# Attention scores as 64 by 64 tiles of the matrix array, with queries loaded contiguous

## The chip, the cores and the metric

The kernel runs on one core of a Trainium2 chip. The metric is device time in microseconds (us) of one execution, the median of several runs. PE is the matrix engine (PEld its weight loads), DVE, ACT and POOL are the vector, scalar and general engines, SP issues most of the transfers.

## The reference, cut to what matters

Three stages follow each other: attention over a window of 64 positions, a feed-forward layer with a rational activation, and a gated linear unit. All of it is float32.

```python
# q, k, v: (4, 8, 576, 64): batch, heads, positions, head size
scores = scale * np.matmul(q, k.transpose(0, 1, 3, 2))      # scale = 1/8
rel = pos[:, None] - pos[None, :]
mask = (rel >= 0) & (rel < 64)
attn = softmax(np.where(mask, scores, -1e9))                # over the keys
x = heads_joined(np.matmul(attn, v))                        # (2304, 512)

h = x @ w_in                                                # (2304, 2048)
g = (a0 + a1*h + a2*h*h + a3*h*h*h) / (1 + |b0|*|h| + |b1|*h*h + 1e-6)
x2 = g @ w_out                                              # (2304, 512)

out = (sigmoid(x2 @ w_gate) * (x2 @ w_val)) @ w_out2        # d_ff = 1536
```

A query sees itself and the 63 positions ahead of it. So the 64 queries of one chunk of a sequence (576 positions are 9 chunks) need the 128 keys of two chunks: the one before and their own.

## The kernel before, in words

The 2304 tokens are cut into 18 units of 128 tokens, `u` = 0 to 17, and these into five blocks of 512, 384, 384, 512 and 512 tokens (units 0 to 3, 4 to 6, 7 to 9, 10 to 13, 14 to 17). `unit` writes down the attention of one unit; `step1` and `step2` write down the two feed-forward stages of a block, one slice of 128 of the hidden width at a time. Weights come in raw, are taken apart into a high and a low float32r part by ACT, DVE and POOL (names `wraw`, `wt`, `wb`, `w`), and three matmuls (`mm3`, line 744) replace one in float32. In the first phase the second product of a slice is a plain float32 matmul (line 842).

The order of the work is made ahead of time. Each call of `op` records a piece of work with a priority, the engines that can do it with a cost each, and what it needs. `Plan.order` then plays the kernel through with these costs, and emits each piece on the engine and at the place that it finds: so a piece's cost or priority moves others, too. On the chip each engine runs its pieces strictly in that order.

The attention of a unit takes these steps, with the eight heads as four pairs (`HP` = 4; a pair fills 128 partitions, 64 for each head):

- `load_qk` loads queries and keys (SP; the first block's keys from ACT's queue). The queries of a pair and of one chunk of 64 tokens form a 128 by 128 square with the two heads on its diagonal. Off the diagonal it is zero: `off_diagonal` clears those quarters with POOL memsets, in four buffers `qd` for the first block and in one, `q_diag`, for all later units, where they stay zero. The load fills the diagonal in two transfers, each a 64 by 8 by 64 block with runs of 256 bytes.
- `scores(m)` makes the scores of chunk m of the unit (m = 0, 1): four float32 matmuls of 128 by 128 by 128 (line 592), one for each pair of heads, into one bank of PSUM. The rows of the result are 2 heads by 64 queries, its columns the 128 keys. In units 0 to 6 (`on_pe`) a bfloat16 matmul of the mask with the identity (line 590) goes into the bank first; later units add the mask on DVE (`mask`, line 599).
- `peak`, `exps`, `inverse`, `norm` are the softmax (DVE, ACT, DVE, POOL or DVE; lines 607 to 629). `turn` transposes on PE (line 640) up to unit 9, `blocks` on DVE (line 657) from unit 10 on.
- `values` multiplies with v (line 666): 16 float32 matmuls of 128 by 64 by 64, whose results go to partitions 0 to 63 and 64 to 127 in turn, so that each uses one half of the columns of the array.
- `x_hi`, `x_lo` take the result apart into the input of `step1`.

A float32 matmul stands as two records of a weight load and a MATMUL in the trace, so the 4 matmuls of a scores job are 8 records. The pool `a` of PSUM has two banks: scores, transposes and values of units from 4 on use them, as do the val product of `step2` and weights that are taken apart late. Where PE has nothing to do before the first feed-forward matmul, the planner fills in matmuls on a cleared tile (`warm`, line 385).

## Time and profile before

| | |
|---|---|
| median of 3 runs | 958.29 us (957.88 to 958.46) |
| span of the profiled execution | 957.6 us, 13934 instructions |
| PE busy | 936.7 us, 98% of the span |
| DVE, ACT, POOL busy | 687.1, 480.9, 276.4 us |
| chain that ended last, by engine | PE 88%, DVE 6%, ACT 3% |

The profile is that of one execution. Its span runs from the first to the last instruction; its own time was not recorded apart from that, and the median of the runs is 0.7 us above the span. A record's start is observed, the end of a MATMUL is modelled, so the time that a job takes on a busy PE is read from where the next job starts. Busy time is the union of an engine's records.

### The profile page before, as it was taken

To read this page: it belongs to the slowest core of one execution; us is meant where nothing else is said; L and a number is where in the kernel's file an instruction comes from. 1 tells how busy PE (TensorE), PEld (TensorE's weight loads), DVE (VectorE), ACT (ScalarE), POOL (GpSimd) and SP (SyncE) were. 2 spreads that over 40 slices of the span, in tenths; PEclk is the share of its full clock that TensorE was granted. 3 is DMA by queue.
4 is the path that set the end of the run, shared out by engine and by line. 5 is a ranking of instruction groups with operands and counts; after the bars stand their busy time and mean duration, and the time that the engine had idled before them with its cause. 6 is when DMAs were issued, how large, how long until landed. Compare 5 with 4: busy or idle time off the path is not lost.

```text
span 957.6 us, 13934 instructions
## 1 busy us (share of the span) xinstructions
PE 936.7 (98%) x4984; PEld 794.0 (83%) x4984; DVE 687.1 (72%) x1174; ACT 480.9 (50%) x983; POOL 276.4 (29%) x286
## 2 busy tenths in 40 slices
PE   8899988999999999999999999999999999999998
PEld 7756646888899999989999998888888888888886
DVE  6999999999999898886667775988998632222221
ACT  6878875567688776753234435544666310001001
POOL 5576653333465343311111112344312000000000
PEclk9999999999999999999999999999999999999999
DMA  9977898999991257953138873100455520013001
GB/s 265 389 249 246 277 315 307 312 364 327 310 358 46 98 165 253 297 165 100 34 94 282 284 237 129 45 1 23 137 195 197 176 66 23 0 44 110 1 1 44
DMA packets 77476, 166.71 MB, mean 174 GB/s; under 512 B 24992, under 2 KB 34208, under 8 KB 77408
## 3 DMA queue, kind: packets, MB, share of 16 engines
q1 hardware_dynamic: 75296, 164.79, 50.8%
q10 hardware_dynamic: 2112, 1.05, 0.5%
q8 instruction: 39, 0.64, 0.3%
q14 instruction: 29, 0.24, 0.1%
HBM read 121.24 MB, written 44.56 MB: 173 GB/s over the span
## 4 chain that ended last, share of the span: by engine, by line
PE 88%; DVE 6%; ACT 3%; DMA 1%; issue 1%; POOL 1%; DVEq 0%; POOLq 0%; ACTq 0%
PE h L744 34%; PE y L744 30%; PE a L744 14%; PE y L842 4%; DVE et L657 2%; PE a L592 2%; PE a L666 2%; ACT sm L615 1%; DMA cb_raw<-in_moe_b_dram 1%; PE a L385 1%; DVE tg L793 1%; DVE wt L444 0%; PE a L640 0%; DMA qd<-in_q_dram 0%; DVE wt L449 0%
## 5 line engine op out<-in xcount | busy, mean ns | idle before, releaser
L744 PE MATMUL h<-x,w 128*128 128x512 f32 (+1 forms) x1680 | 374.6, 372 | 5.2 <-DVE x L322 1.4
L744 PEld LDWEIGHTS h<-x,w 128*128 128x128 f32 x1680 | 306.9, 188 | 53.4 <-issue 3.6
L744 PE MATMUL y<-g,w 128*128 128x384 f32 (+1 forms) x768 | 163.5, 362 | 0.6 <-POOL g L327 0.6
L744 PE MATMUL a<-x,w 128*128 128x512 f32 (+1 forms) x720 | 158.8, 369 | 0.0
L744 PE MATMUL y<-w,g 128*128 128x512 f32 x648 | 158.6, 392 | 0.0
L934 ACT ACTIVATE sg<-h 128x512 f32<-128x512 f32 (+1 forms) x60 | 33.4, 556 | 238.6 <-PE h L744 236.8
L744 PEld LDWEIGHTS y<-g,w 128*128 128x128 f32 x768 | 138.8, 188 | 16.3 <-POOL g L327 1.1
L744 PEld LDWEIGHTS a<-x,w 128*128 128x128 f32 x720 | 130.6, 188 | 16.9
L744 PEld LDWEIGHTS y<-w,g 128*128 128x128 f32 x648 | 120.4, 188 | 24.1
L793 DVE SCALAR_TENSOR_TENSOR tg<-tg,ca_sb,h 128x512 f32<-128x512 f32 (+1 forms) x160 | 110.0, 690 | 19.1 <-ACT ta L772 13.3
L937 DVE TENSOR_TENSOR sg<-sg,a 128x512 f32<-128x512 f32 (+1 forms) x60 | 37.9, 632 | 118.6 <-PE a L744 118.0
L790 POOL TENSOR_TENSOR tq<-tq,ta 128x512 f32<-128x512 f32 (+1 forms) x56 | 75.5, 1348 | 52.6 <-ACT tq L781 39.5
L799 ACT ACTIVATE tr<-tq,biases 128x512 f32<-128x512 f32 (+1 forms) x80 | 54.2, 679 | 57.2 <-POOL tq L790 48.5
L776 ACT ACTIVATE tg<-h,ca_sb 128x512 f32<-128x512 f32 (+1 forms) x80 | 51.6, 645 | 41.9 <-PE h L744 41.4
L824 DVE SCALAR_TENSOR_TENSOR tg<-tg,ca_sb,tr 128x512 f32<-128x512 f32 (+1 forms) x80 | 67.2, 842 | 1.4 <-POOL tr L821 1.2
L805 DVE SCALAR_TENSOR_TENSOR tq<-tq,tr 128x512 f32<-128x512 f32 (+1 forms) x80 | 56.8, 711 | 11.8 <-ACT tr L802 9.2
L441 POOL TENSOR_SCALAR wraw<-wraw 128x512 f32<-128x512 f32 x55 | 45.8, 840 | 58.4 <-ACT wt L428 38.8
L842 PE MATMUL y<-tg,w 128*128 128x512 f32 x128 | 57.5, 594 | 2.9 <-DVE tg L824 2.8
L657 DVE STREAM_TRANSPOSE et<-sm 32x256 f32<-32x256 f32 x128 | 55.8, 436 | 2.2
L802 ACT ACTIVATE tr<-tr,biases 128x512 f32<-128x512 f32 (+1 forms) x80 | 54.2, 679 | 1.6
L785 POOL TENSOR_SCALAR tq<-ta,cb_sb 128x512 f32<-128x512 f32 (+1 forms) x31 | 25.0, 808 | 94.6 <-ACT ta L772 90.2
L322 DVE CAST g<-sg 128x512 fp32r<-128x512 f32 (+1 forms) x31 | 15.2, 490 | 48.6 <-PE y L744 48.5
(105 smaller groups left out, 1063.9 us busy)
## 6 DMA issues: line engine op xcount, KB each, us to landing
w<-wp SPq DMA_DIRECT2D x30, 512.0 KB, 3.4
wraw<-in_moe_w_out_dram SPq DMA_DIRECT2D x28, 512.0 KB, 6.0
w<-wv SPq DMA_DIRECT2D x26, 512.0 KB, 3.5
w<-wg SPq DMA_DIRECT2D x25, 512.0 KB, 3.5
w<-wo SPq DMA_DIRECT2D x19, 512.0 KB, 3.7
vv<-in_v_dram SPq DMA_DIRECT2D x35, 256.0 KB, 4.2
wraw<-in_moe_w_in_dram SPq DMA_DIRECT2D x16, 512.0 KB, 8.3
wi<-w SPq DMA_DIRECT2D x16, 512.0 KB, 3.1
```

What stands on the lines that cost most here:

```text
L441: nc.gpsimd.tensor_scalar(out=x, in0=x, scalar1=0.0, scalar2=0.0, op0=ALU.mult, op1=ALU.mult)
L657: nc.vector.transpose(out=to[cols, :, rows], in_=at[rows, :, cols])
L744: nc.tensor.matmul(p, lhs(a), rhs(b), start=first and n == 0, stop=last and n == 2)
L776: nc.scalar.activation(out=z["g"], in_=z["h"], func=AF.Copy, scale=ca_sb[:, 3:4])
L790: ENGINES[e].tensor_tensor(out=z["q"], in0=z["q"], in1=z["a"], op=ALU.mult)
L793: return lambda e: nc.vector.scalar_tensor_tensor(out=z["g"], in0=z["g"], scalar=ca_sb[:, m:m + 1], in1=z["h"], op0=ALU.add, op1=ALU.mult)
L799: nc.scalar.activation(out=z["r"], in_=z["q"], func=AF.Ln, scale=LN_SCALE, bias=lnb)
L802: nc.scalar.activation(out=z["r"], in_=z["r"], func=AF.Exp, scale=-1.0, bias=exb)
L805: nc.vector.scalar_tensor_tensor(out=z["q"], in0=z["q"], scalar=1.0 + 1e-6, in1=z["r"], op0=ALU.add, op1=ALU.mult)
L824: nc.vector.scalar_tensor_tensor(out=z["g"], in0=z["g"], scalar=ca_sb[:, 0:1], in1=z["r"], op0=ALU.add, op1=ALU.mult)
L842: nc.tensor.matmul(yacc[b][m][:, :n], w[:, m * P:(m + 1) * P], z["g"], start=f == first_f, stop=f == last_f)
L937: nc.vector.tensor_tensor(out=z["t"], in0=z["t"], in1=z["v"], op=ALU.mult)
```

## The change

The scores of a unit are made in another shape. In place of four matmuls of 128 by 128 by 128 for each chunk there are sixteen for the unit, each of one head (64 partitions, `d`) and one chunk (64 queries, `r`): 64 by 64 weights, 128 keys moving. Head j of a pair sits in partitions 64j to 64j+63, so it uses that half of the array's rows, and goes to its own bank; chunk c goes to partitions 64c to 64c+63 of the bank, and so uses that half of the columns. In units 0 to 6 the two heads are still two jobs, in later units one job that takes both banks at once and goes round the four tiles. The queries are loaded as they lie, one transfer of 128 by 512 with runs of 2 KB for each unit, and nothing is cleared. The masks of a bank now hold two chunks, so there are three of them, `nn`, `fn` and `nf`. A table `SHIFTS` adds a number to the priority of 80 pieces of work.

```diff
+SHIFTS = {
+    17: 6, 20: -7, 39: -4, 58: -3, 66: -4, 70: -4, 76: -6, 77: -8, 109: 2.6, 149: -2, 156: -7, 184: -28, 200: -6,
...
-            o.key = (o.prio, n)
+            o.key = (o.prio + SHIFTS.get(n, 0), n)
...
-    q_diag = const.tile([P, 2 * HP, P], F32, name="q_diag")
+    q_sb = const.tile([P, HP, P], F32, name="q_sb")
...
-        nc.vector.tensor_copy(masks["f"], m)
-        nc.vector.memset(masks["f"][:, 0:64], MASKED)
+        for name, c in (("fn", 0), ("nf", 64)):
+            nc.vector.tensor_copy(masks[name], m)
+            nc.vector.memset(masks[name][c:c + 64, 0:64], MASKED)
         nc.vector.tensor_copy(ident16, ident)
-
-    def off_diagonal(engine, tile):
-        for j in range(2):
-            engine.memset(tile[64 * j:64 * j + 64, :, 64 * (1 - j):64 * (2 - j)], 0.0)
...
-            for r in (slice(0, 64), slice(64, P)):
-                nc.sync.dma_start(out=z["q"][r, :, r], in_=qu[r].rearrange("p (n t) -> p n t", t=64))
+            nc.sync.dma_start(out=z["q"], in_=q[:, HP * c0:HP * (c0 + P)].rearrange("p (i t) -> p i t", t=P))
...
-        def scores(m):
+        chunks = [2 * u + c for c in range(2)]
+        mask_u = masks["".join("n" if c % (S // 64) else "f" for c in chunks)][:, None, :].to_broadcast([P, HP, P])
+
+        def scores(js):
...
-                p = z["p", m] = bank(s_s[m])
-                if on_pe:
-                    nc.tensor.matmul(p, ident16, mask_of(m), start=True, stop=False)
+                for j in js:
+                    z["p", j] = bank(s_s[j])
+                    if on_pe:
+                        nc.tensor.matmul(z["p", j], ident16, mask_u, start=True, stop=False)
                 for i in range(HP):
-                    nc.tensor.matmul(
-                        p[:, i * P:(i + 1) * P], z["q"][:, 2 * i + m], z["k"][:, i, 64 * m:64 * m + P],
-                        start=not on_pe, stop=not on_pe or i == HP - 1,
-                    )
+                    for c in range(2):
+                        r = slice(64 * c, 64 * c + 64)
+                        for j in js:
+                            d = slice(64 * j, 64 * j + 64)
+                            nc.tensor.matmul(
+                                z["p", j][r, i * P:(i + 1) * P], z["q"][d, i, r], z["k"][d, i, 64 * c:64 * c + P],
+                                start=not on_pe, stop=not on_pe or i == HP - 1,
+                            )
...
-                            z["et"][:, c, i, 64 * j:64 * j + 64],
+                            z["et"][:, j, i, 64 * c:64 * c + 64],
...
-            o = sc = op(
-                t(j), [pe(512, 4 + on_pe)], scores(j), [lk, zeros, sc, gate],
-                [s_s[j]] + [sm_s][j:], {q_s, k_s}, None if first_block or j else prev_k.get("t"),
-            )
+            if on_pe:
+                sc = op(
+                    t(j), [("PE", 1.4)], scores((j,)), [lk, sc, gate], [s_s[j]] + [sm_s][j:], {q_s, k_s},
+                    None if first_block or j else prev_k.get("t"),
+                )
+            elif j == 0:
+                sc = op(t(0), [("PE", 1.15)], scores((0, 1)), [lk, gate], [*s_s, sm_s], {q_s, k_s}, prev_k.get("t"))
+            o = sc
```

Lines behind the edits shift: the feed-forward matmuls stand at 745 and 843 in place of 744 and 842.

Three places show what moves. The first is SP's queue at the start of the program; `qd` and `q` are the queries of the first block, `ca_sb` and `cb_raw` the coefficients of the rational function, and a bracket names the earlier transfer that a transfer waits for. Before:

```order
L552 DMA qd<-in_q_dram 64x8x64 x4
L373 DMA ca_sb<-in_moe_a_dram 128x4 [waits DMAHW0_49]
L374 DMA cb_raw<-in_moe_b_dram 128x2 [waits DMAHW1_49]
L552 DMA qd<-in_q_dram 64x8x64 [waits DMAHW2_49]
L552 DMA qd<-in_q_dram 64x8x64 [waits DMAHW3_49]
```

And in the changed kernel:

```order
L556 DMA q<-in_q_dram 128x512 x2
L378 DMA ca_sb<-in_moe_a_dram 128x4
L379 DMA cb_raw<-in_moe_b_dram 128x2
L556 DMA q<-in_q_dram 128x512 [waits DMAHW0_49]
L556 DMA q<-in_q_dram 128x512 [waits DMAHW1_49]
```

Two transfers stand ahead of the coefficients in place of four, and the coefficients wait for no earlier transfer.

The second place is PE's order where the first phase of block 0 ends (lines 842 and 843 are its last products) and its second phase begins (`x_1526` and `x_1516` are its input); the scores and transposes between them belong to units 4 and 5. Before:

```order
L842 MATMUL y<-tg,w 128x512 x4
L640 MATMUL a<-ident,sm 128x128 x8
L590 LDWEIGHTS ident_97
L590 MATMUL a<-maskn,ident_97 128x512
L592 MATMUL a<-kt,q_diag 128x128 x4
L590 LDWEIGHTS ident_97
L590 MATMUL a<-maskn,ident_97 128x512
L592 MATMUL a<-kt,q_diag 128x128 x4
L842 MATMUL y<-tg,w 128x512 x4
L744 MATMUL h<-x_1526,w 128x512 x12
```

And in the changed kernel:

```order
L843 MATMUL y<-tg,w 128x512 x4
L640 MATMUL a<-ident,sm 128x128 x4
L843 MATMUL y<-tg,w 128x512 x4
L640 MATMUL a<-ident,sm 128x128 x4
L586 LDWEIGHTS ident_97
L586 MATMUL a<-masknn,ident_97 128x512
L592 MATMUL a<-kt,q_sb 64x128 x8
L586 LDWEIGHTS ident_97
L586 MATMUL a<-masknn,ident_97 128x512
L592 MATMUL a<-kt,q_sb 64x128 x8
L745 MATMUL h<-x_1516,w 128x512 x12
```

The last product has moved up between the two transposes of unit 4, and the scores of unit 5 have moved behind it, next to the first matmul of the second phase.

The third place is PE's order at unit 7, the first without the mask on PE, in the second phase of block 0 (`h` and `a` are the gate and val products, `y` the output product). Before:

```order
L744 MATMUL a<-x_1526,w 128x512 x12
L592 MATMUL a<-kt,q_diag 128x128 x4
L744 MATMUL y<-w,g 128x512 x12
L592 MATMUL a<-kt,q_diag 128x128 x4
L744 MATMUL h<-x_1526,w 128x512 x12
L666 MATMUL a<-et,vv 64x64 x16
```

And in the changed kernel:

```order
L745 MATMUL h<-x_1516,w 128x512 x12
L592 MATMUL a<-kt,q_sb 64x128 x16
L745 MATMUL y<-w,g 128x512 x24
L666 MATMUL a<-et,vv 64x64 x16
L745 MATMUL a<-x_1516,w 128x512 x12
```

Two jobs of 4 matmuls with a product between them have become one job of 16, and 24 matmuls of an output product follow it before a bank of `a` is written again.

## Rows read from the trace of the kernel before

**Rows 1.** The page, busy time, share of the span and instructions of each engine.

```profile
PE 936.7 (98%) x4984; PEld 794.0 (83%) x4984; DVE 687.1 (72%) x1174; ACT 480.9 (50%) x983; POOL 276.4 (29%) x286
```

**Rows 2.** Windows of 24 us: busy us and records of each engine, clock, DMA share.

```profile
24.00:48.00 24.00, 21.24 (x173) 17.65 (x172) 23.58 (x35) 19.78 (x36) 13.08 (x14) 1.00 0.98 389
...
48.00:72.00 24.00, 21.78 (x66) 13.04 (x65) 21.63 (x33) 18.28 (x31) 17.05 (x15) 0.93 0.72 249
...
120.00:144.00 24.00, 20.05 (x68) 10.63 (x66) 22.42 (x36) 17.66 (x41) 13.56 (x13) 1.00 0.92 314
144.00:168.00 24.00, 20.68 (x91) 15.46 (x92) 22.61 (x43) 13.88 (x35) 8.62 (x7) 1.00 0.83 306
...
192.00:216.00 24.00, 24.00 (x149) 19.96 (x148) 22.20 (x38) 15.88 (x42) 7.58 (x8) 1.00 0.98 365
```

**Rows 3.** Timeline of PE: start, us, line, record, count [idle before].

```profile
197.09 1.15 PE L666 MATMUL a<-et,vv 128*64 128x64 f32 x32
198.17 3.02 PE L744 MATMUL y<-w,g 128*128 128x512 f32 x12
201.03 2.89 PE L744 MATMUL a<-x,w 128*128 128x512 f32 x12
203.75 0.60 PE L640 MATMUL a<-ident,sm 128*128 128x128 f32 x4
...
210.15 1.05 PE L592 MATMUL a<-kt,q_diag 128*128 128x128 f32 x8
...
213.78 1.05 PE L592 MATMUL a<-kt,q_diag 128*128 128x128 f32 x8
```

**Rows 4.** Line 666 from 196 to 199 us: record ns min/median/max, first and last start.

```profile
L666 PE MATMUL a<-et,vv x32: 222/222/270, 197.1 to 198.0; 128*64 128x64 f32 x32
```

**Rows 5.** Groups by shape: busy us, mean ns | idle before.

```profile
L629 DVE TENSOR_TENSOR sm<-sm,su 128x512 f32<-128x512 f32 x20 | 14.0, 698 | 0.5
L599 DVE SCALAR_TENSOR_TENSOR sm<-a,maskn 128x512 f32<-128x512 f32 x20 | 13.7, 683 | 5.0 <-PE a L592 5.0
```

**Rows 6.** Timeline of all engines from 0 to 11 us.

```profile
0.73 2.75 SPq L552 DMA_DIRECT2D qd<-in_q_dram  x4
...
2.63 0.59 DVE L361 COPY maskf<-maskn 128x128 bf16<-128x128 bf16 x1 [1.54 <-POOL maskn L357]
...
4.96 0.34 SPq L374 DMA_DIRECT2D cb_raw<-in_moe_b_dram  x1
5.05 0.63 PE L590 MATMUL y<-maskf,ident 128*128 128x512 bf16 x1
...
6.93 1.13 PE L592 MATMUL y<-qk,qd 128*128 128x128 f32 x8 [1.25 <-DMA qd<-in_q_dram]
...
8.83 0.17 DVE L609 TENSOR_SCALAR mx<-mx 128x4 f32<-128x4 f32 x1
...
10.61 0.20 ACT L1047 ACTIVATE cb_sb<-cb_raw 128x2 f32<-128x2 f32 x1 [6.34 <-DMA cb_raw<-in_moe_b_dram]
10.72 0.35 ACT L615 ACTIVATE sm<-y,mx 128x128 f32<-128x128 f32 x1
```

**Rows 7.** DMA issues of the page: KB each, median us from issue to landing.

```profile
vv<-in_v_dram SPq DMA_DIRECT2D x35, 256.0 KB, 4.2
```

**Rows 8.** Timeline of PE from 48 to 155 us.

```profile
53.54 4.14 PE L744 MATMUL h<-x,w 128*128 128x512 f32 x10 [0.37 <-DVE w L327]
...
142.15 0.63 PE L640 MATMUL a<-ident,sm 128*128 128x128 f32 x4 [1.56 <-DVE sm L629]
144.45 0.66 PE L640 MATMUL a<-ident,sm 128*128 128x128 f32 x4 [1.67 <-POOL sm L629]
...
147.46 3.70 PE L842 MATMUL y<-tg,w 128*128 128x512 f32 x8
...
152.56 0.50 PE L744 MATMUL h<-x,w 128*128 128x512 f32 x1 [1.40 <-DVE x L322]
154.40 2.80 PE L744 MATMUL h<-x,w 128*128 128x512 f32 x11 [1.34 <-DVE x L327]
```

More of the change, by code (lines that the diff above doesn't have):

```diff
@@ L58 @@
 HOP = {e: dict(zip(HOP, h)) for e, h in HOP.items()}
+SHIFTS = {
[7 rows of a table added]
+}
 class Plan:
@@ L331, in tile_window_attention__rational_ffn__glu @@
     ident16 = const.tile([P, P], BF16, name="ident16")
-    masks = {m: const.tile([P, P], BF16, name=f"mask{m}") for m in ("n", "f")}
-    q_diag = const.tile([P, 2 * HP, P], F32, name="q_diag")
+    masks = {m: const.tile([P, P], BF16, name=f"mask{m}") for m in ("nn", "fn", "nf")}
+    q_sb = const.tile([P, HP, P], F32, name="q_sb")
     ca_sb = const.tile([P, 4], F32, name="ca_sb")
@@ L348, in constants @@
         nc.vector.memset(two, 2.0)
-        m = masks["n"]
+        m = masks["nn"]
         nc.vector.memset(m, 0.0)
@@ L360, in constants @@
             )
-        nc.vector.tensor_copy(masks["f"], m)
-        nc.vector.memset(masks["f"][:, 0:64], MASKED)
+        for name, c in (("fn", 0), ("nf", 64)):
+            nc.vector.tensor_copy(masks[name], m)
+            nc.vector.memset(masks[name][c:c + 64, 0:64], MASKED)
         nc.vector.tensor_copy(ident16, ident)
-    def off_diagonal(engine, tile):
-        for j in range(2):
-            engine.memset(tile[64 * j:64 * j + 64, :, 64 * (1 - j):64 * (2 - j)], 0.0)
-    def clear_diagonal(e):
-        off_diagonal(ENGINES[e], q_diag)
     def coefficients(e):
@@ L544, in load_qk @@
         def load_qk(e):
-            qu = q[:, HP * c0:HP * (c0 + P)]
             if first_block:
+                z["q"] = tile_of(q_s, [P, HP, P], name="q")
                 z["k"] = spare[0][:, :, c0:c0 + 64 + P]
             else:
-                z["q"] = q_diag
+                z["q"] = q_sb
                 z["k"] = tile_of(k_s, [P, HP, 64 + P])
-            for r in (slice(0, 64), slice(64, P)):
-                nc.sync.dma_start(out=z["q"][r, :, r], in_=qu[r].rearrange("p (n t) -> p n t", t=64))
+            nc.sync.dma_start(out=z["q"], in_=q[:, HP * c0:HP * (c0 + P)].rearrange("p (i t) -> p i t", t=P))
             if first_block:
@@ L568, in load_v @@
             nc.sync.dma_start(out=z["v"][:, 1], in_=v[c0:c0 + P, :])
-        def take_q(e):
-            z["q"] = tile_of(q_s, [P, 2 * HP, P], name="qd")
-        def clear(e):
-            off_diagonal(ENGINES[e], z["q"])
-        def mask_of(m):
-            name = "n" if (2 * u + m) % (S // 64) else "f"
-            return masks[name][:, None, :].to_broadcast([P, HP, P])
-        def scores(m):
+        chunks = [2 * u + c for c in range(2)]
+        mask_u = masks["".join("n" if c % (S // 64) else "f" for c in chunks)][:, None, :].to_broadcast([P, HP, P])
+        def scores(js):
             def go(e):
-                if m == 0:
+                if 0 in js:
                     z["sm"] = tile_of(sm_s, [P, 2, HP, P], name="sm")
@@ L600, in mask @@
                 out=z["sm"][:, c], in0=z["p", c].rearrange("p (i t) -> p i t", i=HP), scalar=scale,
-                in1=mask_of(c), op0=ALU.mult, op1=ALU.add,
+                in1=mask_u, op0=ALU.mult, op1=ALU.add,
             )
@@ L690, in t @@
             return t0 + x
-        ready = zeros = cleared
-        if first_block:
-            ready = op(-360 + u, [("NONE", 0.0)], take_q, [taken], [q_s])
-            zeros = op(-350 + u, [("POOL", 1.1, *PORT)], clear, [ready], uses=[q_s])
         lk = op(
-            prio_load, [dma((1690 if first_block else 1792) * 4 * P, 2.6 if first_block else 3)], load_qk, [ready, near],
-            [x for x in (q_s, k_s) if not first_block], {q_s, k_s}, prev_k.get("k"),
+            prio_load, [dma((1690 if first_block else 1280) * 4 * P, 1.6 if first_block else 2)], load_qk,
+            [taken if first_block else None, near], [q_s] if first_block else [q_s, k_s], {q_s, k_s}, prev_k.get("k"),
         )
@@ L702, in unit @@
         tu = []
-        sc, tr = None, None
+        tr = None
+        sc = None
         for j in range(2):
-            o = sc = op(
-                t(j), [pe(512, 4 + on_pe)], scores(j), [lk, zeros, sc, gate],
-                [s_s[j]] + [sm_s][j:], {q_s, k_s}, None if first_block or j else prev_k.get("t"),
-            )
+            if on_pe:
[6 more added lines that the diff above has]
+            o = sc
             if not on_pe:
@@ L1042, in tile_window_attention__rational_ffn__glu @@
     taken = op(-300, [("NONE", 0.0)], take_spare, takes=[spare_slot])
-    cleared = op(-60, [("POOL", 2.0, *PORT)], clear_diagonal)
     for u in range(UB[0]):
```

6 rows, old and new, of the table SHIFTS are left out of this document.

## The prediction, made before the changed kernel ran

> **What bounds the kernel now.** I read the page first, for which engine is full. PE is busy for 98% of the span [rows 1], so only what shortens PE's own work, or the waits in its missing 2%, can move the end. Next the windows of 24 us over the whole span, for where those 2% lie; five of the 40 stand here [rows 2]. PE lacks 2.8 and 2.2 us in the two windows from 24 us, 4.0 and 3.3 us in the two from 120 us. From 168 us on the windows are full, as the one from 192 us, but for scraps and the end, and what PE saves there comes off the end, if the others keep up. DVE is the one to watch: 23.6 of 24 us busy in the window from 24 us, still 22.2 in the one from 192 us. ACT and POOL have room throughout. So early on DVE and PE share the bound, later PE stands alone.
>
> **Scores in units 7 to 17, the main term.** The reader needs what a job costs on a full PE, from start to start. Twelve 512-column matmuls of the feed-forward take 203.75 - 201.03 = 2.72 us [rows 3]. A scores job of before and the twelve of the product behind it take 213.78 - 210.15 = 3.63 us, so the job costs 0.91, a record of it 0.114, and the two jobs of a unit 1.82 us.
>
> The new shape, 64 by 64 weights with 128 columns moving, is nowhere in the trace. Its nearest row is that of the values, which use half of the array's columns in turn: they and twelve matmuls take 201.03 - 197.09 = 3.94 us, so values cost 1.22 us [rows 3]. Their group lasts 1.15 us, and its last record 0.22 of this, so the 32 starts lie within 0.93 us [rows 3, 4]; the other 0.29 us go into entering and leaving. A record of 64 columns should take half of 0.114 us; 32 in a row would need 1.82, and start within half of that. So the two column halves do work at the same time, at full gain.
>
> The new job has 16 matmuls, 32 records of 128 columns. The bounds: if all four tiles overlap, 32 x 0.114 / 4 = 0.91, and with 0.29 for entering and leaving 1.20 us. If only two do, 1.82 + 0.29 = 2.11. If none do, 3.65 + 0.29 = 3.94. I take 1.20: column halves overlap in the row of the values, and the two row halves here read other partitions and write other banks, so nothing that the column halves share is shared more. That saves 0.62 us a unit, 11 x 0.62 = 6.8 us. Eight of these units lie where PE alone is full; units 7 to 9 lie where DVE has some 2 us free in 24.
>
> The rule that speaks against the change is that of the Trainium skill, "TensorEngine Tiling (Array Packing)", section Tiling Modes: a change of the tiling mode drains the engine. The trace agrees in that the values pay 0.29 us beside their records. By the rule alone, without that price, the sum could not be made; by the row it is in the sum already.
>
> **Scores with the mask on PE, units 0 to 6.** Here a job holds one head, so one row half, and only columns can overlap: 16 records x 0.114 / 2 + 0.29 = 1.20 us against 0.91, 0.29 us more for each job (the mask matmul ahead is unchanged). If nothing overlaps, 2.11, 1.2 us more. The two jobs of unit 6 stand in full PE work: +0.6. The four of units 4 and 5 lie in the stretch from 126 to 155 us, where PE waits for other engines anyway; I count them at nothing, 1.2 us if those waits are gone. Of the eight in block 0 only the first is on the path.
>
> **The start.** The first exponential runs at 10.72 us on ACT, though its row maximum is ready at 8.83 + 0.17 = 9.00 us [rows 6]. What ends last is `cb_raw`: ACT stands in order at the absolute value of it until 10.61, since SP issues it at 4.96, behind four query transfers and a wait for an earlier one. In the new order two transfers stand ahead and no wait. Two issues at 2.75 / 4 = 0.69 us each (the price of the four now), and one of 0.34 ahead of it, bring it to some 2.5 us; with the same 10.6 - 5.0 = 5.6 us on its way it is there at 8.1. The first scores wait until 6.93 for the second query transfer. One of 256 KB takes 4.2 us from issue to landing where it is v [rows 7], so 4.9, and the mask matmul, which ends at 5.05 + 0.63 = 5.68, is then the last. So scores 1.25 us earlier, 0.29 longer, maximum at 8.0, and the first exponential near 8.2, 2.5 us earlier than now. POOL's ten clears go, and nothing takes their place on the path; the extra mask costs DVE one more copy of 0.59 us ahead of the identity, which PE reaches at 5.05 behind its warm-up in both. From there the work runs through ACT's exponentials, POOL, DVE and PE to the first feed-forward matmul. Upper bound 2.5; lower bound nothing, as DVE is 98% busy from 24 us on and has the weights to prepare. I take 2.0, near the upper, as ACT's chain is most of it.
>
> **The moved pieces.** Of 80 shifted priorities I price what the order shows where PE waits. Between 142 and 155 us PE waits 1.56 and 1.67 us for the softmax ahead of two transposes, then runs the last product of the phase (3.7 us), then waits 1.40 and 1.34 us for that product's results to be taken apart [rows 8]. In the new order the product lies between the transposes, and two scores jobs (some 2.9 us with masks) lie where the 1.40 and 1.34 were. Upper bound 1.67 + 1.40 + 1.34 = 4.4 us. Lower bound nothing: the product began at 147.46, after both transposes, so if its factor on DVE comes no earlier, PE only waits in another place. I take 2.0, some 70% of the later two waits. Queued behind the moved product are the second transpose and unit 5's scores; unit 4's values come later and wait for neither at once.
>
> Eight of the normalisations (0.698 us each on DVE [rows 5]) move from POOL to DVE, 5.6 us in all, and other copies leave DVE for ACT in about the same amount. I count this at nothing, covered by those; without that cover it is a rival below. The 28 later query transfers become 14 on a queue with time to spare.
>
> **The clock.** Ten matmuls from 53.54 us took 4.14 us [rows 8], where ten at 2.72 / 12 take 2.27; the granted clock of that window is 0.93 [rows 2], full speed but for a spell at half of it, after PE had waited. That is 1.9 us, which may go, stay or come elsewhere as waits move. Taken as unchanged.
>
> **The sum.** -6.8 (units 7 to 17) + 0.6 (unit 6) - 2.0 (start) - 2.0 (moved product) = -10.2 us. Span 957.6 - 10.2 = 947.4, and with the 0.7 us by which the median of the runs stands above the profiled span, 948.1 us. The forecast's own range is 943 (upper bounds of both early gains and the clock spell gone: 0.5 + 2.4 + 1.9 = 4.8 less) to 953.5 (both early gains nothing, units 4 and 5 paid: 5.2 more).
>
> **Rivals.** First, the row halves take turns. A float32 matmul is two records for the same tile, and if matmuls start in order, the second holds the next tile back, so that only two tiles work at a time: 2.11 us a unit, and 11 x 0.29 = 3.2 lost in place of 6.8 gained: 958.1 us. The change would then not do what it says. The row of the values fits this reading as well as the other. The Trainium skill, "TensorE: Matmul & The Clock Gate", Part 3, says of packed matmuls that they keep strict program order in start and end; by that rule it would come out so. The same part reports row and column packing that multiply, and no run here shows which holds for pairs of records. 12 in 100.
>
> Second, slower: the four tiles do not overlap at all, 3.94 us a unit. It loses 11 x 2.12 = 23.3 us, and 2.4 in unit 6: some 980 us. It decides once a unit's scores cost more than 2.3 us, since the gains elsewhere are 3.4. The values speak against it, as their halves overlap. 5 in 100, and 2 for slower in other ways.
>
> Third, the new job takes both banks of `a` at once, and PE waits for the masks: DVE needs 0.683 us for each [rows 5], and may be at something else. At 0.7 us a unit it is 7.7 us, so 955.8. Against it: in the order of unit 7 24 matmuls follow before the pool is used, and masks had to wait for PE (5.0 us), so DVE is mostly there. 8 in 100.
>
> Fourth, the early gains do not come, as DVE sets the pace up to 310 us: 952.1 us, or 953.7 when the moved normalisations are not covered. 23 in 100.
>
> **How the numbers follow.** The forecast has 50 in 100. A measurement of this kernel can tell 0.2%, 1.9 us, from no change. Faster: forecast, third and fourth, 81. Same: the first, 12. Slower: 7. The range reaches from 943 to 957.5, and leaves out the first and second rivals and little below.
>
> **What would show it.** Line 592 in units 7 to 17: from its start to the next job's, 1.2 us for 32 records (right), 2.1 (first rival), 3.9 (second). The 4.0 and 3.3 us that PE lacks in the windows from 120 us should come to about 5 together. The first exponential on ACT should start near 8.2 us. New waits of PE for line 599 would show the third rival. The prediction is wrong if the row halves take turns, or if DVE takes back what the start gives.

## The result, and the profile after

The changed kernel takes 948.27 us in the median (947.19 to 949.13, 4 runs), the kernel before 958.18 on the same chip (957.88 to 958.46): a ratio of 0.9892, 95% interval 0.9879 to 0.9905. That is faster, by 9.9 us, where 948.1 was forecast.

The profiled execution has a span of 947.3 us against 957.6, and its own time is 949.13. In every execution of these runs for which both are known the time lies 1.7 to 2.3 us above the span. The 0.7 us that the prediction added set the span of one execution against the median of others; an error of about 1 us, within what the spans differ by between executions. One execution of six of a later run, `tile_by_tile`, was a slow one (978.92 us) and is left out; all other numbers are of fast executions.

First the page of the changed kernel, the part that answers to [rows 1]: busy time, share of the span and instructions of each engine.

```profile
PE 930.8 (98%) x5254; PEld 779.7 (82%) x5254; DVE 684.8 (72%) x1177; ACT 479.2 (51%) x989; POOL 260.1 (27%) x267
```

PE is busy for 5.9 us less, and stands still for 16.5 us in place of 20.9. The 5.9 is not the matmuls saved alone: PE counts as busy when it runs at half clock, as the next view shows. The windows of [rows 2], and the one from 264 us, of the changed kernel:

```profile
48.00:72.00 24.00, 21.23 (x63) 12.54 (x61) 21.42 (x33) 18.87 (x32) 14.30 (x15) 0.93 0.79 285
...
120.00:144.00 24.00, 21.30 (x82) 10.65 (x81) 23.41 (x38) 16.84 (x39) 11.76 (x12) 0.94 0.80 285
144.00:168.00 24.00, 23.89 (x124) 18.24 (x123) 21.47 (x41) 15.50 (x35) 6.18 (x7) 0.99 0.81 278
...
264.00:288.00 24.00, 22.60 (x179) 21.34 (x179) 22.07 (x40) 20.04 (x52) 11.27 (x11) 1.00 0.78 290
```

The last of these windows in the kernel before:

```profile
264.00:288.00 24.00, 24.00 (x164) 22.62 (x163) 22.00 (x35) 19.52 (x44) 16.64 (x14) 1.00 0.91 347
```

From 120 to 168 us PE lacks 2.7 and 0.1 us, where it lacked 7.3 in all. But the granted clock of the window from 120 us has fallen from 1.00 to 0.94: a spell at the lower of PE's two levels (1.2 GHz, half speed) is there that was not there before. In the window from 264 us PE lacks 1.4 us, and lacked nothing before. (Windows of two traces that stand at the same time do not hold quite the same work, as the changed kernel is some us ahead.)

The timeline of PE in the changed kernel (start, us, line, record, count, idle before) shows the new jobs and these waits:

```profile
138.79 0.63 PE L640 MATMUL a<-ident,sm 128*128 128x128 f32 x4 [1.31 <-DVE sm L629]
140.81 5.40 PE L843 MATMUL y<-tg,w 128*128 128x512 f32 x8 [1.39 <-DVE tg L825]
146.05 0.60 PE L640 MATMUL a<-ident,sm 128*128 128x128 f32 x4
...
184.67 0.39 PE L586 MATMUL a<-masknn,ident 128*128 128x512 bf16 x1
184.99 1.09 PE L592 MATMUL a<-kt,q_sb 64*64 64x128 f32 x16
186.01 0.39 PE L586 MATMUL a<-masknn,ident 128*128 128x512 bf16 x1
...
206.18 1.10 PE L592 MATMUL a<-kt,q_sb 64*64 64x128 f32 x32
207.21 5.78 PE L745 MATMUL y<-w,g 128*128 128x512 f32 x24
212.92 1.15 PE L666 MATMUL a<-et,vv 128*64 128x64 f32 x32
...
272.35 1.10 PE L592 MATMUL a<-kt,q_sb 64*64 64x128 f32 x32
274.86 2.35 PE L745 MATMUL h<-x,w 128*128 128x384 f32 x12 [1.40 <-DVE tg L794]
...
395.82 1.10 PE L592 MATMUL a<-kt,q_sb 64*64 64x128 f32 x32
396.85 2.35 PE L745 MATMUL h<-x,w 128*128 128x384 f32 x12
```

A job with 32 records (206.18, both heads, four tiles) takes as long as one with 16 (184.99, one head, two tiles): 1.10 and 1.09 us, and from first to last start 0.83 and 0.82. That alone shows that row halves overlap as column halves do. The job of unit 7 and 24 products take 212.92 - 206.18 = 6.74 us; 24 products are 5.44 by [rows 3], so the job costs 1.3, a little of it the entry into the values behind.

The start in the changed kernel, for [rows 6] (timeline of all engines):

```profile
2.12 0.43 SPq L379 DMA_DIRECT2D cb_raw<-in_moe_b_dram  x1
...
5.13 1.09 PE L592 MATMUL y<-qk,q 64*64 64x128 f32 x16
...
7.00 0.17 DVE L609 TENSOR_SCALAR mx<-mx 128x4 f32<-128x4 f32 x1
...
8.47 0.20 ACT L1047 ACTIVATE cb_sb<-cb_raw 128x2 f32<-128x2 f32 x1 [4.29 <-DMA cb_raw<-in_moe_b_dram]
8.58 0.35 ACT L615 ACTIVATE sm<-y,mx 128x128 f32<-128x128 f32 x1
```

`cb_raw` still ends last, 2.1 us earlier than before; the row maximum is ready 1.3 us ahead of it.

To see where the 10 us come from, the starts of the k-th feed-forward matmul (of 3944) were set side by side in two traces. The rows are places up to which all have done the same number of feed-forward matmuls of each kind: the plain float32 products of the first phase take about twice the time of the others, and their order has changed. How many us earlier than in the kernel before the matmul starts, in the changed kernel, and in the one whose table of shifts is empty (`no_shifts`, below):

```
k      us in before   changed   no_shifts   what lies between this row and the one above
0           33          2.39       0.69     the start
256        117          2.17      -0.79     first phase of block 0, all but its end
360        163          4.56      -3.43     end of that phase, units 4 and 5, moved product
480        195          4.05      -2.64     unit 6
960        309          3.90      -5.63     units 7 to 9
1440       392          3.90      -6.17     (no scores here)
2280       577         10.47       0.61     units 10 to 17
3943       953         10.47       0.61     (no scores here)
```

At 163 us `no_shifts` has also done the values of one more unit, 1.1 us of its lag there.

### The profile page after: what moved, and what is told of

It reads as the page before. It is cut to its first block, busy times and chain, and to the rows that moved or that the text cites. A ratio compares the mean times of both kernels' runs of the same rounds, so it can differ in the third digit from the quotient of the medians.

```text
span 947.3 us, 14418 instructions
## 1 busy us (share of the span) xinstructions
PE 930.8 (98%) x5254; PEld 779.7 (82%) x5254; DVE 684.8 (72%) x1177; ACT 479.2 (51%) x989; POOL 260.1 (27%) x267
## 3 DMA queue, kind: packets, MB, share of 16 engines
q10 hardware_dynamic: 2112, 1.05, 0.4%
## 4 chain that ended last, share of the span: by engine, by line
PE 87%; DVE 7%; ACT 3%; issue 1%; DMA 0%; POOL 0%; ACTq 0%; DVEq 0%; POOLq 0%
PE h L745 34%; PE y L745 30%; PE a L745 15%; PE y L843 5%; ACT sm L615 2%; PE a L666 1%; PE a L592 1%; DVE et L657 1%; DVE tg L794 1%; DVE wt L454 1%; DVE tq L806 1%; DVE wt L449 1%; DVE tg L825 1%; DVE w L338 0%; PE a L640 0%
## 5 line engine op out<-in xcount | busy, mean ns | idle before, releaser
L446 POOL TENSOR_SCALAR wraw<-wraw 128x512 f32<-128x512 f32 x54 | 43.0, 802 | 53.3 <-ACT wt L433 29.7
L843 PEld LDWEIGHTS y<-tg,w 128*128 128x128 f32 x128 | 24.5, 194 | 30.5 <-issue 25.5
```

The lines of the kernel that those rows point to most:

```text
L446: nc.gpsimd.tensor_scalar(out=x, in0=x, scalar1=0.0, scalar2=0.0, op0=ALU.mult, op1=ALU.mult)
L843: nc.tensor.matmul(yacc[b][m][:, :n], w[:, m * P:(m + 1) * P], z["g"], start=f == first_f, stop=f == last_f)
```

## The experiments

All start from the changed kernel, whose median is 948.27. The kernel before took 957.98 to 958.18 in the median beside each of them, so the chips that they ran on agree. Where only the order is edited, `behind(where, moved...)` takes pieces out of the finished plan, by their numbers, and puts them behind another; every other piece keeps its place and engine.

```
                  median us   ratio to before (95%)    against 948.27
rows_in_turn       952.66     0.9949 (0.9937-0.9961)      +4.4
columns_in_turn    954.85     0.9973 (0.9964-0.9983)      +6.6
tile_by_tile       965.50     1.0078 (1.0066-1.0090)     +17.2
coefs_late         952.77     0.9956 (0.9940-0.9972)      +4.5
product_late       956.96     1.0006 (0.9983-1.0029)      +8.7
no_shifts          959.16     1.0007 (0.9998-1.0016)     +10.9
fill               946.94     0.9884 (0.9868-0.9900)      -1.3
merged             948.35     0.9893 (0.9879-0.9906)      +0.1
h_later            948.84     0.9899 (0.9884-0.9914)      +0.6
warm52             946.83     0.9884 (0.9871-0.9897)      -1.4
no_idle            945.93     0.9874 (0.9859-0.9888)      -2.3
best               945.34     0.9869 (0.9856-0.9882)      -2.9
```

### Do four tiles overlap, and by what order

```diff
# rows_in_turn
-                for i in range(HP):
-                    for c in range(2):
+                for j in js:
+                    for i in range(HP):
+                        for c in range(2):
...
# columns_in_turn
-                for i in range(HP):
-                    for c in range(2):
+                for c in range(2):
+                    for i in range(HP):
...
# tile_by_tile
-                for i in range(HP):
-                    for c in range(2):
-                        r = slice(64 * c, 64 * c + 64)
-                        for j in js:
+                for c in range(2):
+                    for j in js:
+                        for i in range(HP):
+                            r = slice(64 * c, 64 * c + 64)
```

> The changed kernel, but in each scores job of units 7 to 17 all 8 matmuls of head 0 (upper half of the array's rows) come first, then the 8 of head 1: neighbours in order then differ in columns only. Theory (four tiles work at once, and only as neighbours in the order): a job costs some 2.1 us in place of 1.2, 11 x 0.9 = 9.9 us, so about 958 us, or 956 if units 7 to 9 hide theirs behind DVE. Rival (each tile has a queue of its own, so that the order of the tiles does not matter): no change, 948. Rival (the gain comes from elsewhere, the row halves never overlapped): no change, 948.

> The same for the other half: in each scores job of units 7 to 17 all 8 matmuls of chunk 0 (lower half of the columns) come first, then the 8 of chunk 1: neighbours differ in rows only. Theory (row halves overlap as well as column halves, by neighbours in the order): 2.1 us a job, some 958 us (956 to 959), as with the rows in turn. Rival (row halves do not overlap): 3.9 us a job, 11 x 2.7 = 30 us more, 978. Rival (order does not matter): 948.

> The changed kernel, but in each scores job of units 7 to 17 the four matmuls of one tile follow one another, then those of the next tile (order c, j, i). Theory from the two half orders, where the second half started after 8 of the first half's 16 records (PE starts a matmul of a free tile some records ahead of its turn): one tile's 8 records take 0.87 us, and if the next tile starts when its turn is 8 records away, all four start nearly at once and the job costs 1.2 to 1.6 us: 948 to 952 us. Rival (only neighbours in the order overlap, and the half orders gained at the border alone): near 3.4 us a job, 11 x 2.2 = 24 us more, 972.

Both half orders slow the kernel, so the order matters, and the rivals of 948 and of 978 us fall: neighbours that differ in rows overlap as well as neighbours that differ in columns. But the price was half of the 0.9 us expected. The job of unit 10 in the timeline of PE, first with the rows in turn, then tile by tile:

```profile
397.55 1.59 PE L592 MATMUL a<-kt,q_sb 64*64 64x128 f32 x32
399.07 2.35 PE L745 MATMUL h<-x,w 128*128 128x384 f32 x12
```

```profile
402.13 2.56 PE L592 MATMUL a<-kt,q_sb 64*64 64x128 f32 x32
404.62 2.35 PE L745 MATMUL h<-x,w 128*128 128x384 f32 x12
```

From its start to the next matmul it takes 1.52 and 2.49 us, where the changed kernel takes 1.03. Why is seen in the starts of its 32 records (ns from one to the next, as the traces have them):

```
changed           7 6 7 140 7 6 7 89 7 6 7 89 7 7 6 89 7 7 6 90 6 7 7 89 6 7 7 89 7 6 7
rows_in_turn      7 153 7 102 7 102 7 103 6 6 7 90 6 57 7 39 7 56 7 39 7 56 7 103 6 103 6 103 7 102 7
tile_by_tile      160 109 109 109 6 103 57 52 57 53 56 109 6 104 56 53 56 53 57 109 6 103 57 52 57 52 57 109 109 109 110
```

In the changed kernel four records start within 20 ns, and the next four 109 ns after them (160 the first time): all four tiles work at once. With the rows in turn it is pairs at first, every 109 ns, and after eight records four start together: matmuls of the second half begin while some of the first half's are still to come. In strict order the 16 pairs would need 15 x 0.109 = 1.64 us from first to last start; it was 1.32. Tile by tile, single records start every 109 ns, and the next tile's first record starts 6 ns behind the fifth of a tile's eight; with the rows in turn it is the fifth as well. So PE takes a matmul for a free tile ahead of its turn, but only from there on, and not at once as expected for that run: 965.5 us, which is neither the theory's (948 to 952) nor the rival's (972). Eleven jobs of 1.46 us more are 16.1 us of PE. Of these the traces show 13.5 between unit 6 and unit 17, as waits that the changed kernel has took up the rest; another 3.8 lie ahead of unit 7, where the order changes too.

With the rows in turn 11 x 0.49 = 5.4 us were added to PE, and the traces differ by 3.7 between unit 6 and unit 17: the wait at 274.9 us shrinks from 1.40 to 0.90, other waits take up the rest. The order by columns and that by tiles also hold for the one-head jobs of units 0 to 6, which the expectations did not say: each of them is 0.49 us longer, and by columns the first feed-forward matmul comes 2.2 us later than in the changed kernel. Hence the 2 us between the two half orders.

### The start

```diff
# coefs_late
+behind(64, 85)      # 64: queries of unit 3; 85: coefficients
```

> The changed kernel with one edit of the order: the two coefficient transfers are issued behind all four query transfers, as in the kernel before, and wait there for an earlier transfer; all else keeps its order. Theory (the start is a chain through ACT's exponentials that reaches the end): the first exponential starts near 10.7 us again, 2.1 later, the first feed-forward matmul 1.5 to 2.2 later, and the end 1.5 to 2.2 later, 949.8 to 950.5 us. Rival (DVE sets the pace early, and the start is lost): less than 0.7 us later at the end.

The coefficients came 1.35 us later, not 2.1 (the timeline; then the wait of PE that follows; then windows of 3 us with the clock in the third column from the right):

```profile
9.93 0.35 ACT L615 ACTIVATE sm<-y,mx 128x128 f32<-128x128 f32 x1
...
11.46 0.38 PE L586 MATMUL y<-masknn,ident 128*128 128x512 bf16 x1 [0.80 <-ACT sm L615]
```

```profile
12.00:15.00 3.00, 3.00 (x25) 2.04 (x22) 2.90 (x7) 2.64 (x16) 2.08 (x2) 0.54 0.93 309
15.00:18.00 3.00, 3.00 (x25) 2.23 (x25) 2.52 (x9) 3.00 (x17) 0.80 (x1) 0.50 1.00 385
18.00:21.00 3.00, 3.00 (x21) 2.44 (x17) 1.98 (x6) 1.43 (x6) 1.44 (x3) 0.50 1.03 422
```

PE then stood still for 0.80 us, and ran at half speed from 12 us to past 21; why for so long behind so short a wait, no run shows. The first feed-forward matmul is 4.0 us late, the 120th 3.6, and from there to the end it stays 3.6: nothing of the start is lost, nor made up. So the theory on the start holds, and the size has a second part, the clock. One execution of the six had the mean clock of the changed kernel's profile (0.996; the others 0.987 to 0.991). It took 950.53 us, 1.4 above that profile's 949.13, which is what the coefficients alone explain.

### The moved product

```diff
# product_late
+behind(1046, 1003, 1006, 1009, 1012, 1004, 1005, 1010, 1007, 1013, 1011, 1008, 1014)
+# 1046: second scores job of unit 5; 1003 to 1012: the product; the others take its results apart
```

> The changed kernel with one edit of the order: the last product of the first phase of block 0 and what takes its results apart go back behind the second transpose of unit 4 and the scores of unit 5, as in the kernel before. Theory (the moved product is worth some 2 us): PE waits some 1.5 to 3 us more between 136 and 156 us, and the end comes 1 to 3 us later, 949.3 to 951.3. Rival (the product only moved the waits about): within 0.7 us of 948.3.

It is worth four times the expected (two of the eleven executions even took 966.6 us, at the same mean clock of 0.990 as most others; what held those two is not known). The timeline of PE with the product late, and windows of 4 us:

```profile
138.71 0.63 PE L640 MATMUL a<-ident,sm 128*128 128x128 f32 x4 [1.32 <-DVE sm L629]
143.99 1.11 PE L640 MATMUL a<-ident,sm 128*128 128x128 f32 x4 [4.65 <-DVE sm L629]
...
149.81 6.43 PE L843 MATMUL y<-tg,w 128*128 128x512 f32 x8
...
160.46 3.02 PE L745 MATMUL a<-x,w 128*128 128x512 f32 x12 [1.05 <-ACT sm L615]
```

```profile
140.00:144.00 4.00, 0.01 (x1) 0.01 (x1) 3.93 (x8) 1.38 (x3) 1.09 (x2) 0.71 0.55 196
144.00:148.00 4.00, 4.00 (x24) 2.61 (x26) 1.83 (x3) 0.58 (x1) 0.00 (x0) 0.50 0.98 322
148.00:152.00 4.00, 4.00 (x19) 2.63 (x20) 0.00 (x0) 0.08 (x1) 0.00 (x0) 0.50 0.54 185
152.00:156.00 4.00, 4.00 (x7) 1.53 (x6) 0.74 (x2) 1.17 (x3) 0.00 (x0) 0.58 0.30 98
```

Without the product PE waits 4.65 us for the softmax ahead of the second transpose. Then it runs at half speed from 144 to 155 us, and DVE, ACT and POOL stand idle for its results. The wait is 3.3 us more than the one ahead of the product in the changed kernel (1.39); the half clock, which there lasts only from 141 to 144.5 us, and a further wait of 1.05 us make up the rest of the 8.1 us between the traces. In the changed order the transpose's factor comes from DVE, not from POOL as before [rows 8]: the product that moved up covers a wait that the new order itself has.

### The table of shifts as a whole

```diff
# no_shifts
-SHIFTS = {
...
+SHIFTS = {}
```

> The changed kernel with an empty table of shifts, so that the planner lays out the whole order by itself, with the new scores and the new query loads. Theory (new scores and start give most, the shifts the moved product and a few waits): the scores' 6 us and the start's 2 stay, the rest goes: 950 to 954 us. Rival (the shifts give nothing): 948.3. Rival (the order of the table is what makes the new shape pay): 957 or more.

No faster than the kernel before. The longest waits of PE in this kernel, by what it waited for (us in total, times, longest; its lines stand 8 higher, as the table is gone):

```profile
PE y L835 <- DVE tg L817: 7.3, 4, 3.6
PE h L737 <- ACT ta L765: 3.7, 3, 1.9
PE h L737 <- ACT w L323: 1.7, 1, 1.7
```

The longest of the changed kernel of these kinds (it has none for `ta`):

```profile
PE y L843 <- DVE tg L825: 2.8, 2, 1.4
PE h L745 <- DVE tg L794: 2.4, 2, 1.4
PE h L745 <- ACT w L331: 1.7, 1, 1.7
```

The 959 us speak for the second rival, but the table of starts above says why, and that is another reason: from 392 us on, through units 10 to 17, this kernel gains 6.8 us on the kernel before, as the changed one does (6.6). What it loses it has lost by 309 us, where it is 5.6 us behind the kernel before. From the first feed-forward matmul up to there PE stands still for 16.8 us, mostly for DVE and ACT, where the kernel before has 12.0. So the new shape pays without the table; it is the order that the planner lays out by itself that is worse in the first third, and the shifts take that back and some more. Which of the new costs, the new transfers and the longer one-head jobs spoils the order was not taken apart. Nor was a table fitted to the kernel before, so no run tells what part of the 10 us such a table would have given there.

### The clock, and what is left

```diff
# fill (in turn)
-                for i in range(HP):
-                    nc.tensor.transpose(p[:, i * P:(i + 1) * P], z["sm"][:, j, i], ident)
+                for i in range(HP * (4 if u == 4 and j == 0 else 1)):
+                    nc.tensor.transpose(p[:, i % HP * P:(i % HP + 1) * P], z["sm"][:, j, i % HP], ident)
...
# warm52 (in hidden)
+            for _ in range(7 if (p, f) == (0, 4) else 0):
+                nc.tensor.matmul(h, xt[b][:, 0, 0, 0:P], xt[b][:, 0, 0, :n], start=True, stop=True)
...
# no_idle: fill, warm52, and in values
+            for _ in range(5 if u == 0 else 0):
+                warm_up(e)
```

> The changed kernel, but the first transposes of unit 4 are done four times in place of once, some 1.3 us more matmuls in the wait of 1.39 us ahead of the moved product; nothing else changes. Theory (the half-speed clock from 141 to 144.5 us in the changed kernel's profile follows from PE standing still just ahead of it): the granted clock stays at full speed there, and the kernel is 1 to 2 us faster, 946.3 to 947.3. Rival (the clock falls for another reason): the spell stays, and the time is 948.3 or up to 0.3 more.

> The changed kernel with the second of those places alone: seven matmuls on the block's input in the wait of 1.7 us ahead of the fifth hidden product. Theory: the half-speed spell at 52 to 56 us, which the kernel before had too, goes, and the time is 1.2 to 1.9 us less, 946.3 to 947.1. Rival (the spell comes from elsewhere, or the fillers hold the next product up): 948.3 or more.

> The changed kernel with idle time of PE filled at three places, by matmuls whose results are overwritten or not read: five warm-up matmuls ahead of unit 0's values (a wait of 1.2 us at 17.7 us), seven on the block's input ahead of the fifth hidden product (1.7 us at 48.8), and the repeated transposes of unit 4 (1.39 us at 139.4). Theory (half-speed spells come where PE stood still, some of them in some executions only, and cost 1.5 to 2 us each): the granted clock is full from 15 us on, 943.5 to 945 us in the median, and the executions lie within 1 us of each other. Rival (the spells come anyway): 946 to 947, as with one filled place.

The windows of 3 us around the filled transposes, and the product behind them on PE, in `fill`:

```profile
138.00:141.00 3.00, 2.88 (x15) 1.68 (x13) 3.00 (x4) 1.19 (x2) 1.48 (x2) 1.00 0.53 175
141.00:144.00 3.00, 3.00 (x22) 1.68 (x22) 2.93 (x7) 1.82 (x4) 0.00 (x0) 1.00 0.78 266
```

```profile
139.11 3.70 PE L843 MATMUL y<-tg,w 128*128 128x512 f32 x8
```

In this execution the clock is full, and the product takes 3.70 us in place of 5.40; the traces differ by 1.53 us at this place. In `warm52` the first place is at full clock, and the second, not filled there, is not:

```profile
51.00:54.00 3.00, 1.95 (x7) 1.30 (x8) 2.96 (x6) 1.84 (x3) 1.01 (x1) 1.00 0.97 348
...
141.00:144.00 3.00, 3.00 (x6) 1.10 (x5) 2.93 (x7) 1.10 (x2) 0.00 (x0) 0.67 0.67 218
```

Over the traces of all runs that keep the table of shifts: near 140 us the nine in which that wait is not filled all have a spell, the three in which it is filled (`fill`, `no_idle`, `best`) have none. Near 52 us six of nine have one, and none of the three with that place filled (`warm52`, `no_idle`, `best`). So the spells follow PE's standing still there, the first of them not each time. Each execution's time and mean granted clock (a spell of 3.4 us at half speed takes 0.002 from the mean) show how they come and go:

```
changed    949.13 0.996   949.00 0.996   947.19 0.998   947.55 0.998
fill       945.85 1.000   949.19 0.996   948.04 0.997   945.79 1.000
warm52     947.87 0.998   946.23 0.999   947.42 0.998   945.86 0.999
no_idle    946.29 1.000   945.69 1.000   946.14 0.999   945.72 0.999
```

A spell is worth about 1.7 us, and by these means the changed kernel has one in some of its executions and two in others. Filling one place does not keep spells away: two executions of `fill` lost as much clock as the changed kernel, at places that no trace shows, and its four reach over the range of the changed kernel's, so that the gain of `fill` rests on the traces more than on its median. With PE kept busy at three places the spells of the profile are gone, and the executions lie within 0.6 us. The medians of `fill` and `warm52` lie within their forecasts; the 945.93 is just above its 943.5 to 945, which had been made from spans. In the kernel before no such worth is seen in the whole time: its executions with a mean of 1.000 took 957.3 to 959.7 us, those with 0.996 957.1 to 958.4.

```diff
# merged (in scores)
+                both = u in (5, 6)
...
-                        for j in js:
+                        for j in js if not both else () if js == (0,) else (0, 1):
...
# h_later
+behind(1256, 1302)      # 1302: the waiting hidden product; 1256: the output product behind it
```

> The changed kernel, but in units 5 and 6 the two one-head jobs of scores become one that goes round all four tiles: the first job only writes its mask, the second its mask and all sixteen matmuls. Theory (sixteen matmuls on four tiles cost as much as eight on two): 1.2 us of PE saved in unit 6, which stands in full PE work, and up to 1.2 in unit 5: 946 to 947.2 us. Rival (holding the bank longer or a later softmax makes another engine wait): 948.3 or more.

> The changed kernel with one edit of the order: the hidden product that waits 1.40 us behind unit 9's scores, at 274.9 us, goes behind the output product that followed it. Theory (that wait took back what units 7 to 9 save): 0.8 to 1.4 us faster, 946.9 to 947.5. Rival (DVE is late there anyway, and the wait moves to the next product): 948.3.

Neither theory held in size. The joined jobs save PE 2.0 us in the two units together. But the second mask now waits for its bank, and a product behind unit 5's scores waits longer for an exponential (0.65 us for 0.11), 1.55 us more in all (timeline of PE in `merged`), and the traces differ by 0.4:

```profile
147.16 0.38 PE L586 MATMUL a<-masknn,ident 128*128 128x512 bf16 x1 [0.46 <-ACT et L331]
...
152.16 3.03 PE L746 MATMUL a<-x,w 128*128 128x512 f32 x12 [0.65 <-ACT sm L616]
...
185.44 0.38 PE L586 MATMUL a<-masknn,ident 128*128 128x512 bf16 x1 [0.55 <-DVE sg L939]
```

Moved behind the output product, the hidden product no longer waits, but the output product does, for ACT and DVE to copy the results of the block before out of its bank, as the timeline of PE in `h_later` shows:

```profile
272.62 1.32 PE L745 MATMUL y<-g,w 128*128 128x384 f32 x6 [0.17 <-ACT osb L331]
274.46 1.31 PE L745 MATMUL y<-g,w 128*128 128x384 f32 x6 [0.52 <-DVE osb L333]
```

In the traces 0.35 us are left at this place, and the median shows nothing. DVE is what is late there.

> The three filled places together with the joined scores jobs of units 5 and 6 and the hidden product moved behind the output product at 275 us. Theory (the pieces add): 0.6 to 1 us less than with the filled places alone, 943 to 944.3 us. Rival (each of the two only shifts a wait): the same as with the filled places alone.

945.34 us, with a ratio of 0.9869 (0.9856 to 0.9882): the fastest here, 2.9 us below the changed kernel, and above the 943 to 944.3 of its forecast. The joined jobs and the moved product give 0.7 us in the traces on top of the filled places, about the sum of what each gave alone (0.4 and 0.35), and 0.6 in the medians, at the edge of what these runs can tell.

## Why the prediction was right, and where its steps were off

**Scores in units 7 to 17: right in mechanism, near in price, and -6.4 for -6.8 in part by luck.** A job was to cost 1.20 us if all four tiles overlap. From its start to the next start it is 1.03; what the products behind it lose comes on top, by the way that [rows 3] was read: the gap between the feed-forward matmuls on either side of a job is 1.40 us on average in units 10 to 17, of which one such matmul is 0.17 to 0.23: 1.2. The 0.91 + 0.29 that were read from the values [rows 3, 4] hold in both parts: records at a quarter of 0.114 us, and the rest for entering and leaving. But the gain was not spread as thought. In units 7 to 9 the scores took some 1.4 us less for the 1.9, and the lead did not grow at all (-0.15), as PE now waits 1.40 us behind unit 9's scores for DVE, which the prediction had called free enough. Units 10 to 17 gave 6.57 where 5.0 were forecast. Counted from start to start, scores and the products behind them are 4.5 of this, even with a stall of 0.5 us that unit 16's job now has inside; the other 2.1 are waits for POOL and DVE at the values of units 10, 11 and 17 and a product ahead of them, 2.6 us before and 0.5 now. The prediction had taken PE as full there, so that these 2.1 us are luck, and make up for units 7 to 9.

**The rivals.** That row halves take turns fell: four records start within 20 ns. The Trainium skill, "TensorE: Matmul & The Clock Gate", Part 3, holds matmuls to strict program order in start and end; its table there, in which packing in rows and in columns work together, is what the trace agrees with. Strict order does not hold here: with the rows in turn it takes 1.32 us from first to last start, where strict order needs 1.64, and as a tile's records stand at least 109 ns apart, at most ten of the first half's sixteen can have started when the second half does. The rival's price of 2.11 us a job, from strict turns, was too high too: even with the rows in turn a job costs some 1.7. The third rival, new waits for the masks, fell with one such wait of 0.1 us, at 250.6 us. DVE's busy time fell from 687.1 to 684.8 us, so the normalisations that moved to it were covered, as the prediction had assumed.

**Unit 6: right,** a lead smaller by 0.5 for +0.6. A one-head job with its mask takes 186.01 - 184.67 = 1.34 us in the profile.

**The start: right in size, and not by the loads alone.** The first feed-forward matmul came 2.4 us earlier for the 2.0 taken (1.7 to 2.5 in the traces of other runs whose start is the same, 0.8 in that of `rows_in_turn`, which has a half-speed spell from 19 us), and what is lost at the start is lost at the end, as the delayed coefficients show. The first exponential came at 8.58 for 8.2: `cb_raw` was issued at 2.12 for 2.5, but took 6.35 us for the 5.6. So the fourth rival, that DVE sets the pace and the early gains are lost, fell. But without the shifts, with the same loads at the same places and the first exponential at 8.99, the first feed-forward matmul came only 0.7 us earlier than before: about 1 us or more of the term needs the new order behind the loads, for which the prediction has no term.

**The moved product: right in size, from two misses that cancel.** From 117 to 163 us the lead grew by 2.4 us, for -2.0. PE lacks 2.8 us in the windows from 120 us, where the prediction looked for 5 and the kernel before lacked 7.3; so the waits shrank by 4.5 us. But the clock spell from 141 us took 1.5 of this back (`fill`), and the longer scores jobs of units 4 and 5, counted at nothing as covered by waits, 0.6, now that most of the waits are gone. Taken back in the new order the product costs 8 us, not 2: a wait's worth in the order before says little of what it covers in the order after.

**The clock was taken as unchanged, and was not.** The spell that the kernel before has at 54 us stayed, and a second one came behind two waits of 1.31 and 1.39 us. Why there is open: the kernel before has waits of 1.56 and 1.67 us as close together [rows 8], and its clock stayed full there (1.00 from 120 to 168 us [rows 2]). The prediction named that a spell may come elsewhere, and priced only the gain, if the old one went. Its 1.9 us were read from the length of the ten matmuls, the end of which is modelled; from their start to the next start it is 3.98 us, so 1.7, which is what the runs give for a spell.

**Not priced at all:** the worth of the table, 10.9 us, as the prediction read only the places where PE waits in the order of before. The sum came out right all the same, since it compared the two orders that ran. It would have been wrong as a statement on what each part of the change is worth: the new scores and loads by themselves, with the planner's own order, leave the time where it was.

By stages the sum is 2.4 (start) - 0.2 (first phase) + 2.4 (moved product, less the new spell) - 0.5 (unit 6) - 0.15 (units 7 to 9) + 6.6 (units 10 to 17) = 10.5 us at the last matmul, and 10.3 between the spans, for a forecast of 10.2. The mechanisms hold, that of the start only with the new order behind it; that the medians meet within 0.2 us is luck, as misses of up to 2 us in single stages cancelled.

## What to carry to other kernels

In this kernel small float32 matmuls gain in full from 64 by 64 tiles when neighbours in the order go round the four tiles; with one half after the other, or tile by tile, much of it is lost (1.03, 1.52, 2.49 us for the same 16 matmuls). Where a planner sets the order, a cheaper operation changes the whole order: compare the stage that is full with the stages that wait, and do not credit the edit with what the order gives or takes. When you set two traces side by side by the k-th matmul, see to it that both have done the same work up to there. Where PE is the bound, a wait of a microsecond can cost twice, once as a wait and once as a half-speed spell behind it; work that is thrown away, put into the wait, bought some 1.5 us in the traces at each of two places, 1.3 and 1.4 in the medians.

## What was not expected of the hardware

A matmul for a free tile starts ahead of its turn, but not at once: in both orders together with the fifth of the eight records of the tile that is at work, some 0.49 us after that tile's first. So the strict order in which an engine runs its pieces does not hold for PE's records inside a piece.

PE's half-speed spells are partly a matter of the single execution: the one at 52 to 56 us stands in the changed kernel's profile, and not in that of `fill`, though the waits ahead of it are the same in both (PE is busy for 1.3 of the 3 us from 48 us in both). In `product_late`, after 4.65 us of standing still, the clock stayed at half for 11 us of full work.
